# A two-tile head load moved to GpSimd's queue, and the key weights one place forward

## The chip, the cores and the metric

The kernel runs on one core of one Trainium2 chip. A core has a matrix engine (TensorE, PE in the profile; its weight loads are the row PEld), VectorE (DVE), ScalarE (ACT), GpSimd (POOL) and SyncE (SP), each with an instruction stream of its own. They meet through semaphores. Data come from device memory (HBM) into on-chip memory (SBUF, 128 partitions) by transfers that SP, ACT or POOL issue, each on a queue of its own; sixteen DMA engines of the core carry out what is queued. The results of matrix products lie in PSUM, eight banks.

The metric is the time of one execution on the device, in microseconds (us); each figure is the median of several runs. The profile is one further execution, recorded by the hardware profiler.

## The reference

Two layers follow one another on an input of 2048 tokens by 512 features: linear attention with 32 heads, then a gated unit that mixes along the tokens. The change touches what comes first, the layer norm of the input and the key product.

```python
def _A_ref(x, wqkv, wo):
    qkv = (x @ wqkv).reshape(B, S, 3, H, Dh)     # q, k, v of 32 heads
    pq, pk = phi(q), phi(k)                      # phi(t) = (t + 1 if t > 0 else exp(t)) + 1e-6
    kv, z = einsum('bhsd,bhse->bhde', pk, v), einsum('bhsd->bhd', pk)
    o = einsum('bhqd,bhde->bhqe', pq, kv) / (einsum('bhqd,bhd->bhq', pq, z) + 1e-6)
    return o.reshape(B, S, D) @ wo

def _B_ref(x, w_in, w_sp, b_sp, w_out):
    z = gelu(x @ w_in)
    z1, z2 = z[..., :Fh], layernorm(z[..., Fh:])
    return (z1 * (w_sp @ z2 + b_sp)) @ w_out

h  = x + _A_ref(layernorm(x), wqkv, wo)
h2 = h + _B_ref(layernorm(h), w_in, w_sp, b_sp, w_out)
```

## The kernel before

The program is written as a list of operations. Each has an engine, the tensors that it reads and writes, an estimated cost and, for a transfer, a latency until it lands (`lat`). From the tensors the program derives which operation waits for which; `soft` entries add an order for the planner alone. The order of all operations is not worked out while the kernel is built: it is a permutation, stored as the compressed string `ORDER`. Each engine runs its own operations in the order in which that string has them, and waits (on semaphores) where another engine or a transfer has to be done first.

The input has 16 tiles of 128 tokens. In the head of the program, `k_unit(n)` takes two tiles at a time: statistics on DVE (L544, L545; tile 1's on ACT instead, `ACTS`), the reciprocal root of the variance on ACT (`rstd_act`, tiles 0, 2 and 3) or on POOL (`rstd`, `rpow`), the normalization into `xn` (L589 on DVE for tiles 0 to 5), the transposition, the key product with `wqkv[:, :, D:2D]` into a PSUM bank, `phi` on ACT and DVE into `pk`, and then the product of `pk` with `xn` (L693), which is summed over all tiles. Tiles 0 to 3 are transposed on PE (L603, with `ident` as the operand, then copied by ACT into `xnT`), later ones by transposing transfers on SP's queue. Until tile 0 is there, PE runs products of the zero tile `warm` (L627). `q_unit` (the query product, L435) is placed between the key units; the first one stands after those of tiles 0 to 3.

The order on each engine at the head, as `ORDER` has it:

- SP: loads of tile 0, tile 2, `wka` (key weights, the upper half of the input features), tiles 4 and 5 (one load), tiles 6 and 7, tiles 8 and 9, `wq` (query weights), tiles 10 and 11, then transposes and the other loads.
- ACT: loads of tile 1, tile 3, `wkb` (the other half of the key weights); the load of the exp table (L532); two passes over tile 1 (`sh`); Ln and Exp for tile 0, then for tiles 2 and 3; four copies to `xnT` (tiles 0, 3, 2, 1); `phi`.
- POOL: the memsets of `warm` (L472) and `ident` (L473), the other constants (among them `epst`, which ACT's Ln reads, and `expo`), then small operations for the statistics.
- DVE: statistics of tiles 0, 3, 2; normalization of tiles 0, 3, 2, 1; statistics of tiles 5, 4, 6, 7, with `phi` from tile 0 on among them.
- PE: warm-up, transposes of tiles 0, 3, 2, the key product of tile 0, the transposes of tile 1, the key products of tiles 2, 1, 3, the L693 product of tile 0, the first query product.

`first_load` (L507) makes a head load; its argument `behind` makes the issuing engine wait until another load has landed. So the load of tiles 6 and 7 waits on SP for tile 2 (`x2`), and that of tiles 8 and 9, with those from 10 on, for `wkb` (`wk`).

Of the kernel before, what the change touches and what calls it, by code (L numbers as in the profile page):

```python
# [1261 lines left out]
```

## Time and profile before

| | |
|---|---|
| median of 3 runs | 223.34 us (223.34 to 223.61) |
| the profiled execution | 223.98 us, of which the span is 222.2 |
| granted TensorE clock | 1.0 throughout |
| data moved | 27.12 MB, mean 122 GB/s |

The profile is read from several views. The page gives the busy time of each engine. The chain of waits follows the work that ended last back from the last instruction: at each step to what released it. The timeline lists instructions in order of time, with the idle time in front of each and its releaser in brackets; an engine's name with a q (SPq, ACTq) is its sequencer, which issues transfers. The view of transfers gives for each issue the time until it landed. A table by stretches gives the busy time of each engine and, at its end, the granted clock, the busy share of the DMA engines and their traffic.

### The profile page before, as it was taken

The numbers are of one execution on the slowest core, as the hardware profiler recorded it, in microseconds if no ns is written. First come the engines' busy times: TensorE is split into PE (matmuls) and PEld (weight loads), VectorE is DVE, ScalarE is ACT, GpSimd is POOL, SyncE is SP. The second block draws the span as 40 slices with busy tenths as digits, with TensorE's granted clock in tenths as the row PEclk, the third lists the DMA queues.
The fourth block names the chain that finished last, engine by engine and source line by source line (L and its number), as shares of the span: only waits on it lengthen the run. The fifth ranks groups of instructions, "written<-read, shape, count | busy, mean of one in ns | idle before, by whom it ended". The sixth has DMA issues, their size and how long they took to land.

```text
span 222.2 us, 3893 instructions
## 1 busy us (share of the span) xinstructions
PE 215.9 (97%) x1346; PEld 125.5 (56%) x1358; DVE 207.1 (93%) x484; ACT 142.7 (64%) x283; POOL 49.7 (22%) x133
## 2 busy tenths in 40 slices
PE   8999999999999999999999999999999999999995
PEld 8543444343343554454455556756767798767764
DVE  3899759989998999999999999999999999999995
ACT  5778663277998999999856447626284459423330
POOL 3354500000573693885620000000000000000000
PEclk9999999999999999999999999999999999999999
DMA  6658778965747536303992552998563200433564
GB/s 193 217 121 236 170 167 196 236 137 131 142 101 139 118 71 122 71 0 78 195 139 78 160 126 43 182 189 115 107 119 67 41 1 3 83 73 59 111 190 155
DMA packets 75027, 27.12 MB, mean 122 GB/s; under 512 B 64768, under 2 KB 75008, under 8 KB 75008
## 3 DMA queue, kind: packets, MB, share of 16 engines
q1 hardware_dynamic: 74304, 26.30, 55.9%
q10 hardware_dynamic: 704, 0.59, 0.8%
q8 instruction: 10, 0.16, 0.3%
q14 instruction: 9, 0.07, 0.1%
HBM read 6.95 MB, written 2.10 MB: 41 GB/s over the span
## 4 chain that ended last, share of the span: by engine, by line
PE 79%; DVE 9%; DMA 5%; ACT 3%; SPq 2%; issue 1%; DVEq 0%
PE psum L435 73%; PE psum L693 5%; DMA x<-in_A_x_dram 3%; DVE st L544 2%; DVE pqT L620 2%; DMA zgT<-z1t 1%; DMA r<-rcp 1%; SPq L786 1%; ACT sh L454 1%; ACT e L454 1%; DVE e L615 1%; DVE us L756 1%; DVE h L1198 1%; DVE pqT L810 1%; SPq L465 1%
## 5 line engine op out<-in xcount | busy, mean ns | idle before, releaser
L454 ACT ACTIVATE psum<-psum 128x448 f32<-128x448 f32 (+2 forms) x79 | 32.3, 424 | 29.2 <-PE psum L435 22.7
L435 PE MATMUL psum<-z,wt 128*128 128x448 bf16 (+1 forms) x216 | 41.5, 335 | 0.1
L435 PEld LDWEIGHTS psum<-z,wt 128*128 128x128 bf16 x216 | 20.9, 98 | 15.4 <-ACT z L454 0.3
L435 PE MATMUL psum<-win,hnT 128*128 128x448 bf16 x112 | 25.8, 353 | 0.0
L454 ACT ACTIVATE e<-psum 128x1024 bf16<-128x1024 f32 (+1 forms) x18 | 16.7, 927 | 9.3 <-PE psum L435 8.7
L454 ACT ACTIVATE z1t<-psum 128x448 bf16<-128x448 f32 (+1 forms) x24 | 16.4, 682 | 9.5 <-PE psum L435 8.1
L454 ACT ACTIVATE p<-psum,b 128x448 f32<-128x448 f32 x24 | 14.7, 640 | 6.6 <-PE psum L435 4.2
L435 PE MATMUL psum<-ws,hs 128*128 128x448 bf16 x72 | 18.4, 353 | 0.0
L435 PEld LDWEIGHTS psum<-win,hnT 128*128 128x128 bf16 x112 | 10.7, 98 | 10.4 <-ACT z L454 0.3
L435 PE MATMUL psum<-zt,sa 128*128 128x448 bf16 (+1 forms) x92 | 16.3, 316 | 0.0
L693 PE MATMUL psum<-pk,xn 128*128 128x512 bf16 x62 | 15.4, 380 | 0.3 <-DVE pk L618 0.2
L435 PE MATMUL psum<-xnT,wqkv 128*128 128x512 bf16 x63 | 15.3, 379 | 0.3 <-DVE pqT L620 0.2
L435 PE MATMUL psum<-wqkv,xnT 128*128 128x512 bf16 x62 | 14.9, 379 | 0.7 <-ACT xnT L454 0.4
L435 PE MATMUL psum<-m,pqT 128*128 128x512 bf16 x62 | 14.8, 380 | 0.6 <-DVE pqT L810 0.4
L454 ACT ACTIVATE z<-psum 128x896 bf16<-128x896 f32 x16 | 14.9, 957 | 0.0
L888 DVE TENSOR_TENSOR psum<-psum,p5z 128x448 f32<-128x448 f32 x24 | 14.9, 623 | 0.1
L1038 DVE TENSOR_TENSOR u<-psum,p 128x448 bf16<-128x448 f32 x24 | 14.6, 617 | 0.4 <-ACT p L454 0.2
L568 POOL TENSOR_SCALAR st<-st 128x1 f32<-128x1 f32 x10 | 6.9, 691 | 34.1 <-ACT sh L454 32.6
L544 DVE BATCH_NORM_STATS2 st<-x 128x6 f32<-128x512 bf16 x15 | 9.8, 678 | 4.1 <-DMA x<-in_A_x_dram 4.0
L435 PE MATMUL psum<-wout,zgT 128*128 128x256 bf16 (+1 forms) x72 | 13.0, 297 | 0.1
L435 PEld LDWEIGHTS psum<-zt,sa 128*128 128x128 bf16 x92 | 8.9, 98 | 5.0
L454 ACT ACTIVATE sh<-h 128x512 bf16<-128x512 bf16 x16 | 10.0, 626 | 1.6 <-DVE h L858 1.3
(158 smaller groups left out, 463.7 us busy)
## 6 DMA issues: line engine op xcount, KB each, us to landing
r<-rcp SPq DMA_DIRECT2D x16, 128.0 KB, 2.7
out_dram<-h SPq DMA_DIRECT2D x15, 128.0 KB, 1.8
win<-in_B_w_in_dram SPq DMA_DIRECT2D x4, 448.0 KB, 3.8
x<-in_A_x_dram SPq DMA_DIRECT2D x6, 256.0 KB, 3.7
wqkv<-in_A_wqkv_dram SPq DMA_DIRECT2D x2, 512.0 KB, 4.9
wout<-in_B_w_out_dram SPq DMA_DIRECT2D x1, 896.0 KB, 5.2
wt<-in_B_w_sp_dram SPq DMA_TRANSPOSE x32, 3.7
wo<-in_A_wo_dram SPq DMA_DIRECT2D x1, 512.0 KB, 6.5
```

The costliest lines, as they stand in the source:

```text
L435: inst = pe.matmul(out_ap, lhsT=a, rhs=b, start=start and i == 0, stop=stop and i == len(pairs) - 1, **kw)
L454: return g.add("ACT", lambda ac: ac.activation(out_ap, in_ap, func, **kw), [in_ap, *extra], [out_ap] + ([accum] if accum is not None else []),
L465: return g.add(eng, lambda q: q.dma_start(out_ap, in_ap), [in_ap], [out_ap], cost=issue, lat=lat, dma=name, **k)
L544: dve(lambda v: v.bn_stats(s[:, 0:6], src[:, n, :]), [src[:, n, :]], [s[:, 0:6]], D)
L568: pool(lambda p: p.tensor_scalar(s[:, 2:3], s[:, 0:1], s[:, 0:1], -1.0 / (n * n), op0=ALU.mult, op1=ALU.mult), [s[:, 0:1]], [s[:, 2:3]], 240)
L615: dve(lambda v: v.tensor_scalar(e, e, 1.0, EPS_PHI, op0=ALU.min, op1=ALU.add), [e], [e], w * GW, acc=4)
L620: dve(lambda v: v.scalar_tensor_tensor(dst, t, 1.0 + EPS_PHI, e, op0=ALU.add, op1=ALU.max), [t, e], [dst], w * GW, ps=True)
L693: inst = pe.matmul(bank(CB[c]), lhsT=xn[:, i, c * P:(c + 1) * P], rhs=pk[:, i, :], start=i == 0, stop=i == NT - 1)
L756: return dve(lambda v: v.tensor_tensor(out_ap, a, b, op), [a, b], [out_ap], n, acc=2)
L786: g.add("SP", lambda q: q.dma_start(dst, src_ap), [rcp[:, i:i + w, :]], [dst], cost=700, lat=2200, dma=f"r{tg}{c // 2}")
L888: dve(lambda v: v.tensor_tensor(half(b), half(src), p, ALU.add), [half(src), p], [half(b)], HW, ps=True)
L1038: dve(lambda v: v.tensor_tensor(u, half(b), p, ALU.add), [half(b), p], [u], HW, ps=True)
```

## The change

Tile 2 and tile 3 were two loads of 128 KB, one on SP's queue and one on ACT's. They become one load of both tiles (256 KB) on POOL's queue. It is issued after the memset of `warm` and before that of `ident`. The halves of the key weights thereby become the second load on SP's queue and on ACT's. The load of tiles 6 and 7, which waited on SP for tile 2, waits for the new load. The estimated latencies of the three loads are set anew, and `ORDER` is stored anew for a program of one operation less. Read engine by engine, the new string has the same order as the old one on all five engines, but for the loads named. The two strings are left out here.

```diff
-    queue = {"SP": [], "ACT": []}
+    queue = {"SP": [], "ACT": [], "POOL": []}
...
     load_x("SP", 0, 1, 2150)
     load_x("ACT", 1, 1, 2300)
-    x2 = load_x("SP", 2, 1, 2300)
-    load_x("ACT", 3, 1, 2550)
-    first_load("SP", wqkv[:, 0:2, D:2 * D], A_wqkv[0:2 * P, D:2 * D], "wka", 4200)
-    wk = first_load("ACT", wqkv[:, 2:4, D:2 * D], A_wqkv[2 * P:4 * P, D:2 * D], "wkb", 4400)
+    x2 = load_x("POOL", 2, 2, 3000)
+    x2.soft.add(0)
+    g.ops[1].soft.add(x2.i)
+    first_load("SP", wqkv[:, 0:2, D:2 * D], A_wqkv[0:2 * P, D:2 * D], "wka", 4400)
+    wk = first_load("ACT", wqkv[:, 2:4, D:2 * D], A_wqkv[2 * P:4 * P, D:2 * D], "wkb", 4600)
     for n, lat, behind in ((4, 4600, None), (6, 3400, x2), (8, 3850, wk)):
         load_x("SP", n, 2, lat, behind)
```

More of the change, by code (lines that the diff above doesn't have):

```diff
@@ L15 @@
 SEM_NS = 45.0
-ORDER = "c-jrtg92EG76ibvyXVHXZQE&_G`4Nqww=bdZCh<@+qU)Ie8ogGvj_%@XOS(Eg|JW-)uNcpEv`i~T38D#q=mEimc$ZRUW;x?Eukf{+?LD|TRux}c`TLXw-lDz{<4%-*wR=5D`GJ$trfJQmce3L9V=w9td^y-VwT?OT5W4>^(>QRwEC9C+FEhTY}u@lWwplE#@bm4%W2uIy*03smcu$&1#4*ith9BszpbK$w*J=H%2+82V*@Ogb+SrU)?!;#8)#jus|~WsHrT3J73*e0th!CKq1M#G+dnqK;#d=#WHs!%4YSF%)TUTD8);LmnboxNHqC}xbDM76ZJD*OS=Pg5*lb&DEv=_5vAwq3W?Cy-VY{uDjkcB6+iuz_TWzCkt?jctw#NF{ej8&4Y_6@dLpIjt*g+d-hwX;-wRv{L#@kVwZ|iM=9kUI#&9-5qZMR#t$)4K;duTgsvn{kow$qN=F8kN6+G9Iw*X%!gV)yKfJ+l+G$j;eG+hV(L-Y(h&+iI8WlwGzf_S8PuJ3DP3?WcXRP>6+J_SIfkfNvHXzbynlTU3NZ9DK28AmSo4;sJ<`KNbebV2FXR_+j@gDZ(Kp!Xr5%A_7t)624nxq(K5iL0Y6hUN}-B1L7ke(xE7X^vI7?NQjK6fWJ@-1#s6Aqbw4kAS$8|>YzB1pb|163re6h{zhSBML85fNn}G^ltO)!M`q+gJJdrPR7OrzK?C$fTU133ltwi)M0@l?c2q|{bihcIL2op|RvbZN)WTOZK@HSK9vnqej6r{NL^I^ZzvzSA7>nuXgzXrG0T_p6=!}|}fzcR<Sr~-on2F`+g4?zdT`?Og@C^qr2Q9D)$1oS)aS(Sg7(MVG4q*t6qbF|TFz(?8PGCIlpd04lBv#{<b;o=>z$vuE1pLH9tieRw$4hI4UzmhP7>bMd2e0ihUSSw6Av@RNG~U<(T*f-QMh;%Vdi=&hyuonf<W$7x2>ihrkZ<iRoM(}XSFr&*AihHa#w8e%0ncF(ax)&MAr#N!2@-KKj3Jnqc{l~3`4kCx4Plss&#(lMxft(}hDjNPJ-8WRxe-zM0eRV-oA4278I7M%h!>EKJ$W6^k)KOZm(lqG1(=?n(VO8Ig9TZe`52z{xCOnKfj3ZxG5HrGurP}<BX1%Z8?YFQFe2--A^Wg6V=)t7q8v*wHXE@oTd^OLvoUwFKg%-(cQ7;m<}I{l7FOUcM&dlC<QEKPDpq70?q(d8WLs9^K$hYj4&V@0W@!%M9Jb?pmf<kYWoi!PUJmC%E?^aA<v})KRgT~yR^xkS;{=XmQ!eICyk#>k;Y6-xa~@%P-m!OV!8IJk4qVEPoWuwAfz>&hYxxhC@gqC&Gh6Z#$8Zl0aWdC&ESK{OSMUVab3exME2r=~zi}mxas&V4K5pbx{@^A~<0}5-FHUD!{>uaW&CcA+V;s-JoWXs7w(t+P@g7abN!4H>on;r!<W@?v7|3;or+JDYbdt3gTIp0>A$6BE8A@Gwf#(=T7uk&u8CJ9T-ooh;BPqPD@;oo|4)5~{3oC-I@e%hTqP8=#9<Y|KGm4_=F{A1RpD?<fvW8-)vSMjJW9k|E`%T7H9o=Fa#Z^_^W<ABzb0$=L<=0ClP;S*!BIQwH{iUQzqGEc*;!39adcnVyTqTrO4V6+UR6r$_UJX=AsnkfNRYYl&T18bxnN(Zll}}~WSmktD71Tr(m0fjJNlo>dQ`ADu)Irr$MH$snv(#EM)KLS}MsHY9T{OtEYL$AbliDk-)+n>Os;@U!XJt@7AEcSyO}*4gvwV(bs-3!PuGVRw2CIj9Yo2CnzJ{o+a%r{tXs9-8qh@<Hh4roaPup}t!?Z~|)K?qSPbalN!?jSOG(w9M&bMo%wrIU}YJm6GE{)bQ?bc$A(H;%<oEod4zE{h&L=pU7E!94))P9}PI8D?+t<ZQy^huhar;6kUbVmQ^xXvoE=g?Xm(@~w%R6S8-&!WS6tV4?L=XFaTbwS~Mnr`c&j%c!`>xC{UnSat%UDgnPscX8UE4rbt`l4^TtNZ$)S9-1Qx~X6Ktb6*Y<o-a{^;^UInf{3W{Qnhrt4De$IXv(vKF0_8aDS&%KEji_`v*n!ydKR*d1?>k(S3}M^t2ws(|8IW?HfJ4r}VL&&U1T0pWqpMl8^Hwp2f%eWY6eRe4=OdO#Y9@^tqndbND=;=Gi>EPxnn8+vj^M&+oZ>q5tIzJf|=AIKIg9cma>=3A~^$@xq?SL-<l}=J7nF7xH|*%$NIn74el`!OQvzU*&JK+DrHvFY4=ktN-oAe4DrMI$qq@d2`?HrF@6)_MKkRH+yN{<rV#;@9}cJ#cTV1ujHY9uh;d19>y#CK0o6B`F%g^Q~iM-@Roka%lm0R=4br4*Yh%d*8lYre%{Y{6~E{gyuP>cOa9$k`zgQdKfH}!^@o1NuX_V;>+QX&H}rOX%WwKMzu}Mlu0Qc=e#fi(FMsMC{F%@2NB-QS1YNv_zwoa9(rbB5Z{)AMyZ7+d-qRcVTYuy4y`wkrrvB02`BCrWpZtTz3_AN~|LtG=kAL;G-pwtD8f@@h9xF&2L<?dEy**CQ$KwVJ;s*%g1u=r#?m_e*L7*UAaL*G5LGaU)2H!kkkUR(#qzDoP>4Pvqh#*{$GDs4H4?+gXf($`~AXSh$2pwb$(gb0H%t53eQxGx85=0KN2LA)Me2vi"
@@ new lines @@
+ORDER = "c-jTQ0{|EY5Cp)zz5Up>ZQHgQHnwdxwr!)a)7Z9c+h%8gNQi)lFvLX&gn~mLA|ndIB0xxlLsY~;JS0Xm#77<^K?3ALLL@~ZBtu^0MoJ_{KBPb@<VRtoMsyTF5yU_m6hv(lMS8?UA=E-z)Il-)jaEp9x~PYYXoC#Mj7(^V;>d!mXoS{iixOyuY{-H7Xpd6Jjs~cRzUY852#u2Hgi7d#Fer;yD2<Nz2c3}<l~E2=(H~tf097y$)$kX(Vh{$SI>w_3!Xq{&Vi>NWF(#k}hF}twU^phDJf@%~nxX=RVk)Mg8M<L6mZCYPqdR6{5n7-J7GoD?U>RECU+h3njKp%>KrgJoN{qm2tio>WL~rcDDD1@?tifpP$3D!)7#zTL^ua;Q#aJA|Jgmih9L73qu`O7S|8Nr<@Bq&+4qLGi3-A!za0J_N1xIlek8lQeaSV@f8c(s^j$<Lt;siF~94_EIHsc~r;u0?73Etx^PT>Q7;3Gm>O#6bLcn;ZD{6Z`X>=U9`2#al>5!KA%SSX8YuxR!hp)INXL39ga-*FE~EUd+_aF)y>Sa?fi5$ziyS!#=Kku8lSw>;*S!qQtj%WG+^sL|3{K1*o{EQ3|F{8r2g*c}wKL{`ocS|O`swXL`%wh~s^GFoOUX|1fVm9i{W-bz~$%W8G3o>j0+mebl=YpY^)Er<PO^{uM4u|AgFs#zIpVAU;~wX>eq*BV+`Yj4A?k@d38*4PeO6RTw%?2FZ~ruMhxwnH|``dLTIWxegF?Xb}{&Hl50Y=n)mPPWwgTTPp8BW-|nwwcz<y4Va`X1B21X4${?)%MzKYi=v-u+6b=w$JX^K<jSDY>@4@Bi6%i*#Wz2-)*cNx4CxPy4pNDVJqz=##uMJZzrvV{jgQ`z{cAIyJs)Z(tg@RduW60g1y2cTWv3Gz74U9mW^xdl)c7UyJQROm1XB;`(>wXsJ*r`mV@hTipAqF`)$TIcw=YHdCqe3ifuLWt;J^?f*~j_v|OBOaT$`2Eg>h_9}76y5-~SJ@rfniReNfonV5?$5*OJ!OU)#V%<kN1VYuF+@V(_>H*T;GmWEOJ(F*arJ+rjz!E2U}OYFJTVKf$CI)>#Z>&0-4&P{gR3Nk$ZW?tT~y6nmHtj!3F!Tc=DqRhagjLG^e##k)EdThYnOvd8O$mD!s<(Y{k*oO_7nJw9ujo6Rdn1U6Ul3RJxO0pFzG9tHgE=%#V4P<FnVr!ORS?*wLwqa%V=Re%ZL9D_7oXxhJ$01C`IULNP+{Fd_i}RU<Rk@FiIgATgjqjM1<2am6xQN@VDc`Ue7jryUvN;d39pCacR&fN|a|t_e0^jpKs&gb)vm+;RDL?QNTW}OVa;NR*Xinl9F5_qZ%P~C8wcKN0xSW&ujbFKrhj@&;xt>$_of|lnEBJ%c_>+5Cjz{^68`+76IhF@Fox5!l;lH_scln1$XkLSb{0uvD1~-#FlXCadJjIg?`~+(;lvnq(9>VXiCPR7`p66MH_6zLF2b{$){tjXNA|rY@KgTP)#M`{gdo1kX{VE@FmqqaZ7|HLmmS1CJkLr&Y#jo=*qxloo@aSH}WBMM(@Tcsj8;s?({U+mhY_ICKSl8qFGbZqOp3h$}zUT6qp3rl9BG2zhJh2z^mn`l{y`Dd3Nl)e_JdZc<6rS7*cqvck^}V#G^oCx>i+E~J<wd=$XY{|lg6H*e-pI@QDX-{_J)2kZI$qhE_$yBK=HArXdj_xOe|Za^>8*Uazh(#j$6I?r@9bH8fL3@9@96D3jc4*z-o^W<nWy(o-d6*BhPrxBZ|O5N+h=%N@8)xSjraHNKG1vlT%YChe2};CoW9a~`(WSb>wT88dKhi?W4^_Y`w-vYTfL93^S*w<=lf7!;3IsPFZ8hb&xiXaU+dfaANBL?KGK)^4qxP>e5Vgo4j=7<wab_JVh^vQzQlL?azE*Ne2kCxeg3bH^$42a<NS$7)LuXB6a9#v@kGk*tNpMa^0Pk0AA2Na_5=RN_j^2@^PB#`&wDsc^;>?y5BemZ=Fk12C)G#4;+K4oUiekN?U((!fAP=$)$jN{|L!mSm4EXa{?kACT~DSTe&4V8FCU_({@YE@{Exr!hyK7RNQ$i4>aU@C>nSx%N#uI(QItnfHA1NrQqeR@!<9zSm0HO)QtOpYDKuJXl}iaUPU$s4i8V%<HCB_9L6bFJS(H%|6+?5BN!c}5Q<Y6wHBB27OY;;{`IJ)&lwb3eLyHt!3zb_16i4w@P>WSq2^DCGnkueBsF3n%sg~)T7twN6R5|^t*S<n4RYI#&RBN?aB~?sY)LgYyTx--!|EaXLYKOL|ls2l2wyTm(Xs60+lm6BoRaPkNQXPfXK2_0f9n>-1(*aG<eeG2X?N<ez(qWy}5!F>$9n~2f*EyZlU%H_4s;8E^sBdbele(nuYOO1Jpv$_Z`f8(gs;UNRtDCx^tGcd7x}$1(tlO%tpL(M9daCJqsAq~CbXE;LR~NldE!9**y;L`K*DLi<BfZgUy;BD@Rug^DTOCqIebjr!2s-JLe(AG*>x)*atNtiTuueS{Ge{Fe4Ppho6g%jxIDrN60t9h`=)o;{5G{xwqzxF{RiZ$_4<!k{DnXDe2pOack_QQc&_NJ{4N?S&gK$BJAZd_32p^;jQU#%c3_<E3Opqyv7-S401et?KL6+cu*CLIX"
```

## The prediction

> **What bounds the kernel now.** I read the page first, then the chain of work that ended last, then the timeline of the first 18 us engine by engine, then the landing times of the loads issued there, and last the traffic in stretches of 1 us.
>
> ```profile
> span 222.2 us, 3893 instructions
> ...
> PE 215.9 (97%) x1346; PEld 125.5 (56%) x1358; DVE 207.1 (93%) x484; ACT 142.7 (64%) x283; POOL 49.7 (22%) x133
> ```
>
> TensorE (PE) is busy for 215.9 of 222.2 us, so a change to four loads can only move the point from which that stream runs. The chain shows where this point is set (columns: start, duration, what):
>
> ```profile
> 0.79 0.39 SPq L465
> ...
> 1.25 0.41 SPq L465
> ...
> 2.17 5.98 DMA x<-in_A_x_dram
> ...
> 8.18 1.29 DVE st L544 x2
> ...
> 17.42 1.47 PE psum L435 x6
> ...
> 21.04 1.73 PE psum L435 x8
> ```
>
> From 17.42 us on the chain is PE's, and what starts it is VectorE's (DVE) work from 8.18 on, which waited for tiles 4 and 5 (issued at 2.17, landed at 8.15). A delay or a gain at 17.42 reaches the end whole, since what follows is dependent work with no load of fixed time in it. Eight matmuls take 1.73 us there, so PE can begin one every 0.216 us.
>
> The head itself, by the timeline (start, duration, what, and in brackets the idle time before it with its releaser):
>
> ```profile
> 0.78 0.20 POOL L472 MEMSET warm<- 128x128 bf16 x1 [0.29 <-POOLq L1247]
> 0.93 0.20 POOL L473 MEMSET ident<- 128x128 bf16 x1
> ...
> 1.24 0.45 ACTq L465 DMA_DIRECT2D x<-in_A_x_dram  x1
> ...
> 1.71 0.43 SPq L465 DMA_DIRECT2D wqkv<-in_A_wqkv_dram  x1
> 1.72 0.46 ACTq L465 DMA_DIRECT2D wqkv<-in_A_wqkv_dram  x1
> ...
> 2.03 0.27 POOL L492 TENSOR_SCALAR_AFFINE_SELECT selm<-selm 128x32 bf16<-128x32 bf16 x1
> ...
> 3.96 0.18 DVE L545 BATCH_NORM_AGGREGATE st<-st 128x2 f32<-128x6 f32 x1
> 4.07 0.37 SPq L465 DMA_DIRECT2D x<-in_A_x_dram  x1
> 4.26 1.29 DVE L544 BATCH_NORM_STATS2 st<-x 128x6 f32<-128x512 bf16 x2
> ...
> 4.88 0.28 ACT L454 ACTIVATE rs<-st,epst 128x1 f32<-128x1 f32 x1
> ...
> 5.68 0.38 DVE L589 TENSOR_SCALAR xn<-x,st,rs 128x512 bf16<-128x512 bf16 x1
> ...
> 6.35 1.20 PE L603 MATMUL psum<-ident,xn 128*128 128x128 bf16 x12
> 6.37 1.06 DVE L589 TENSOR_SCALAR xn<-x,st,rs 128x512 bf16<-128x512 bf16 x3 [0.31 <-ACT rs L454]
> ...
> 7.02 0.60 ACT L454 ACTIVATE xnT<-psum 128x512 bf16<-128x512 bf16 x1 [0.69 <-PE psum L603]
> ...
> 7.94 0.81 PE L435 MATMUL psum<-wqkv,xnT 128*128 128x512 bf16 x3 [0.39 <-ACT xnT L454]
> ...
> 9.60 0.66 DVE L544 BATCH_NORM_STATS2 st<-x 128x6 f32<-128x512 bf16 x1
> ...
> 9.67 1.89 PE L435 MATMUL psum<-wqkv,xnT 128*128 128x512 bf16 x8
> ...
> 11.76 1.04 PE L693 MATMUL psum<-pk,xn 128*128 128x512 bf16 x4 [0.19 <-DVE pk L618]
> ```
>
> Two strands run here. **Strand one**: the statistics of tiles 3 and 2 (4.26, in that order on DVE) stand ahead of tile 0's normalization (5.68), so the landing of tile 3 sets tile 0's transposes (6.35), its copy (7.02), the first key matmul (7.94) and the last of the key matmuls (the eight from 9.67). **Strand two**: the landing of tiles 4 and 5 sets DVE's stream from 8.18. The strands meet at PE's matmuls of 11.76, which wait for DVE's keys. PE's last key matmul begins at 9.67 + 7 x 0.216 = 11.18, so PE could go on at 11.40 and has 0.36 us to spare; DVE, idle from 6.37 + 1.06 = 7.43 to 8.18, has 0.75. As the profile stands strand two is ahead by those 0.36 us.
>
> Landing times, each row from the stretch around its issue (last figure: us from issue to landing):
>
> ```profile
> x<-in_A_x_dram ACTq DMA_DIRECT2D x1, 128.0 KB, 3.0
> ...
> wqkv<-in_A_wqkv_dram SPq DMA_DIRECT2D x1, 256.0 KB, 5.7
> wqkv<-in_A_wqkv_dram ACTq DMA_DIRECT2D x1, 256.0 KB, 5.9
> ...
> x<-in_A_x_dram SPq DMA_DIRECT2D x1, 256.0 KB, 4.8
> ...
> x<-in_A_x_dram SPq DMA_DIRECT2D x1, 256.0 KB, 2.7
> ```
>
> Tile 3, issued at 1.24, landed at 4.24, and DVE took it at 4.26. The key weights landed at 7.41 (SP's half) and 7.62 (ScalarE's, ACT's); tile 0's copy ended at 7.02 + 0.60 = 7.62. The 4.8 is tiles 6 and 7 (issued at 4.07, when tile 2 had landed), the 2.7 tiles 8 and 9.
>
> ```profile
> 1.00:2.00 1.00, 0.95 (x10) 0.96 (x11) 0.00 (x0) 0.00 (x0) 0.85 (x9) 1.00 0.10 32
> 2.00:3.00 1.00, 1.00 (x12) 1.00 (x11) 0.00 (x0) 0.80 (x1) 0.30 (x2) 1.00 1.01 327
> 3.00:4.00 1.00, 1.00 (x12) 1.00 (x10) 0.73 (x2) 0.99 (x2) 0.00 (x0) 1.00 0.85 230
> 4.00:5.00 1.00, 1.00 (x12) 1.00 (x11) 0.88 (x3) 0.97 (x5) 0.00 (x0) 1.00 0.88 286
> 5.00:6.00 1.00, 1.00 (x12) 1.00 (x11) 1.00 (x4) 0.57 (x3) 0.74 (x3) 1.00 1.10 365
> ...
> 7.25:8.25 1.00, 0.61 (x8) 0.45 (x7) 0.25 (x2) 1.00 (x3) 0.00 (x0) 1.00 0.07 25
> ```
>
> The last two columns are the DMA engines' busy share and GB/s. Traffic starts just before 2.0 and the engines are then full; but from 7.25 to 8.25 a share of 0.07, one engine of sixteen, is all that runs. So the late landing of tiles 4 and 5 is one engine's backlog, not a lack of bandwidth: by 6.0 us 32 + 327 + 230 + 286 + 365 = 1240 kB had moved of the 1311 kB that end with tile 5. Without that engine's delay they would have landed before 7.43 and strand one would lead.
>
> **The change part by part.** *Removed:* the second issue on SP's queue and the second on ACT's (0.41 and 0.45 us). The key weights move from 1.71 to 1.25, the load of tiles 4 and 5 from 2.17 to 1.71, and ACT's table load begins as much earlier. None of this buys anything by itself: the first key matmul waits for tile 0's copy as much as for the weights; tiles 4 and 5 pay only while strand two leads, 0.36 at most; ACT's work after the table load waits for tile 1, and what it makes is first needed by DVE behind tiles 3 and 2.
>
> *Added on GpSimd (POOL):* one issue between the memset of warm and that of ident, at about 0.95. Behind it stand ten short setup instructions, done at 2.03 + 0.27 = 2.30. Their first users are ACT's Ln at 4.88 (epst) and PE's transposes at 6.35 (ident), so an issue of up to 2.5 us stays covered; without that cover each us more would cost a us on tile 0. The memset of warm, which PE's warm-up waits for, stays ahead.
>
> *Moved behind the pair:* on SP the load of tiles 6 and 7 waits for tile 2, from now on for the pair, and behind it stand the loads of tiles 8 and 9, the query weights, and all later loads and transposes. Issued at 4.8 rather than 4.07 and landing 2.7 to 4.8 later, it is there at 7.5 to 9.6; DVE wants it at 9.60 plus the shift. Nothing.
>
> *The pair itself* is the term that decides. Before, tiles 2 and 3 stood ahead of the key weights in the same two queues; after, they share the engines with them. No row shows a load from POOL's queue, so I bound it. **Below:** DVE is busy with tile 0 until 3.96 + 0.18 = 4.14, so the pair cannot be used over 0.10 sooner than 4.24. **Above:** the nearest rows are 256-KB loads in the same crowd, 4.8 and 5.9, which give 0.95 + 4.8 = 5.75 and 6.85. **Taken:** the three queues carry 262 kB each (tile 0 and half of SP's weights' traffic; the same on ACT; the pair). Shared in thirds all is moved when 786 kB have passed: at 327 GB/s from 2.0 (32 kB before it) 2.31 later, at 4.31; at the traced rates (589 kB by 4.0, then 286) at 4.69. The lag to the landing is that of tile 3: 524 kB had passed at 3.0 + 165/230 = 3.72, it landed at 4.24, 0.52. So 4.8 to 5.2. I take 4.8, since the dip between 3 and 5 falls on a time when two queues changed from one load to the next and a third would fill it. That is 0.56 later than 4.24.
>
> *The Trainium skill speaks against the change here.* Its page "DMA: Bandwidth & Descriptors" (section "Latency and other measured facts") gives a load issued by GpSimd a first byte after about 1 us, one by the other two queues about 0.6; the trace has 1.2 for the latter (0.79 to 2.0), and no run here shows the former. By the page's difference the pair would land at 5.2, an estimate, and the time would be 224.3.
>
> **The sum.** The profiled execution took 223.98 us, 222.20 of it the span. Strand one moves by +0.56. In an execution like the profiled one 0.36 of it goes into PE's spare time (and DVE starts at 7.43 + 0.56 = 7.99, where tiles 4 and 5, due 0.46 earlier at 7.69, no longer hold it): +0.20, 224.18. The median of the runs shown is 223.34, 0.64 below the profiled execution; one without the lagging engine would be 0.36 below it, so I hold that the timed ones mostly lack it. There strand one leads already and the whole +0.56 shows: **223.34 + 0.56 = 223.9**. With the late landing in the timed runs too: 223.34 + 0.20 = 223.54.
>
> **The rivals.**
>
> *The pair is served first.* If POOL's queue gets half of the traffic rather than a third, 262 kB at 327/2 GB/s from about 2.15 are through at 3.75, landed at 4.27: +0.03, no change, 223.3 (223.0 where the late landing is typical and 0.33 of it are saved). For it: nothing stands ahead of the pair in its queue. Against: SP and ACT shared the time evenly, their key weights issued together landing 5.7 and 5.9 later. The skill's same page ("Queues, rings and completion order") says that an engine goes round the queues by whole packets, of some 9 to 17 descriptors; a queue with larger packets would then get more than its third, which no row here can show.
>
> *The faster side: the key weights are what PE waits for.* They land at 7.62, when tile 0's copy ends. If in the timed runs the lagging engine holds them past 7.62 by 0.46 or more, and the pair is not later than 4.24, then PE's first key matmul gains the whole 0.46 by which both halves are issued earlier, and tiles 4 and 5 come with it: 223.34 - 0.46 = 222.9. For it: the two ends coincide within the rows' rounding. Against: it needs the timed runs to lag more than the profiled one, which is the longer one.
>
> *POOL's queue is slow.* If making the transfer's descriptors on POOL, or its place in the crowd, takes as long as tiles 6 and 7 took, the pair lands at 5.75: +1.5, 224.85; with the 5.9 of the weights 6.85: +2.6, 225.95. For it: these are the only 256-KB loads in a full stretch. Against: one lagging engine made them late.
>
> **How the numbers follow.** Forecast 0.46, pair served first 0.21, weights 0.16, slow queue 0.17. About 0.2%, 0.45 us, is what a measurement of this kernel can tell, so slower begins at 223.79. The forecast's own range is 223.5 to 224.3, from the late landing's 223.54 to the skill's and the traced rates' 4.69 + 0.52 = 5.21; I give 0.33 of its 0.46 to slower, the rest to the same. Slower is 0.33 + 0.17 = 0.50; the same 0.13 + 0.21 + 0.02 = 0.36; faster 0.14. The range of 223.0 to 225.0 takes in the forecast, the first rival and the nearer half of the slow queue.
>
> **What would show it.** The statistics of tiles 3 and 2 begin at about 4.8 instead of 4.26, tile 0's normalization at 6.24, the first key matmul at 8.5; the key weights land well before that; DVE has no wait for tiles 4 and 5; PE's matmuls of 11.76 begin without a wait on DVE. Statistics at 4.3 or sooner would be the first rival, a first key matmul released by a load the second, statistics past 5.6 or a setup instruction of POOL holding up ACT's Ln the third. Another order of magnitude in the head, or a difference that arises behind 17.42, would make the whole reading wrong.

## The result and the profile after

| | before | after |
|---|---|---|
| median, same chip | 223.48 us (4 runs, 223.34 to 224.14) | 226.63 us (4 runs, 226.50 to 227.76) |
| ratio, 95% interval | | 1.0138 (1.0119 to 1.0157) |
| the profiled execution, its span | 223.98, 222.2 | 226.50, 224.8 |
| mean granted TensorE clock | 1.0 | 0.992 |

The change costs 3.15 us (226.63 - 223.48), where the forecast was 0.56 and the range ended at 225.0.

The chain of waits of the changed kernel, in order of time (start, duration, what):

```profile
0.79 0.20 POOL warm L472
0.99 0.34 issue
1.33 5.14 DMA x<-in_A_x_dram
...
6.50 1.28 DVE st L545 x2
...
10.34 1.49 PE psum L435 x3
...
12.25 1.93 PE psum L435 x8
...
14.20 0.61 ACT e L454
...
19.23 1.24 DVE pqT L621
...
20.51 1.47 PE psum L435 x6
```

The load in the chain is now the pair, 5.14 us from issue to landing, and the point from which PE's stream runs has gone from 17.42 to 20.51: +3.09. On the way there the chain now passes through PE's key products (10.34 and 12.25) and ACT's `e` (14.20), where before it ran on DVE. Behind the point nothing is lost. From this point to the end of the span it takes 224.8 - 20.5 = 204.3 us, and 222.2 - 17.4 = 204.8 before.

The timeline of the changed kernel's head, from the answers for POOL, DVE, PE and ACT:

```profile
0.79 0.20 POOL L472 MEMSET warm<- 128x128 bf16 x1 [0.29 <-POOLq L1248]
1.33 0.94 POOL L465 DMA_DIRECT2D x<-in_A_x_dram  x1 [0.34 <-issue]
...
3.41 0.27 POOL L492 TENSOR_SCALAR_AFFINE_SELECT selm<-selm 128x32 bf16<-128x32 bf16 x1
...
6.50 1.28 DVE L545 BATCH_NORM_STATS2 st<-x 128x6 f32<-128x512 bf16 x2 [2.20 <-DMA x<-in_A_x_dram]
...
9.59 1.28 DVE L545 BATCH_NORM_STATS2 st<-x 128x6 f32<-128x512 bf16 x2
...
13.41 0.29 DVE L616 TENSOR_SCALAR e<-e 128x512 bf16<-128x512 bf16 x1 [1.15 <-ACT e L454]
...
14.83 0.29 DVE L616 TENSOR_SCALAR e<-e 128x512 bf16<-128x512 bf16 x1 [0.19 <-ACT e L454]
...
8.36 0.40 PE L604 MATMUL psum<-ident,xn 128*128 128x128 bf16 x4 [2.16 <-DVE xn L590]
...
14.86 1.03 PE L694 MATMUL psum<-pk,xn 128*128 128x512 bf16 x4
...
12.29 0.60 ACT L454 ACTIVATE xnT<-psum 128x512 bf16<-128x512 bf16 x1 [1.48 <-PE psum L604]
```

DVE takes the pair at 6.50 instead of 4.26. The statistics of tiles 4 and 5 (9.59) have no wait in front of them any more: their load is there in time. In exchange DVE waits 1.15 and 0.19 us later on, for ACT's `e`, and ACT had waited 1.48 for PE. On PE, 14.86 - 8.36 = 6.50 us lie between the first transposes and the first L694 product; before it was 11.76 - 6.35 = 5.41. What slowed PE is in the table by stretches (stretch, its length, busy time of PE, PEld, DVE, ACT, POOL, then granted clock, DMA share, GB/s):

```profile
2.50:4.50 2.00, 2.00 (x22) 2.00 (x20) 0.88 (x2) 1.41 (x4) 1.03 (x10) 1.00 1.05 344
6.00:8.00 2.00, 0.20 (x4) 0.02 (x1) 1.50 (x5) 0.00 (x0) 0.73 (x2) 1.00 0.13 38
...
9.00:10.00 1.00, 0.92 (x8) 0.92 (x10) 1.00 (x4) 0.66 (x2) 0.00 (x0) 0.54 0.87 229
10.00:12.00 2.00, 1.78 (x9) 0.90 (x8) 2.00 (x6) 0.81 (x2) 0.74 (x2) 0.50 0.90 293
12.00:13.00 1.00, 1.00 (x7) 0.47 (x5) 0.25 (x1) 0.71 (x2) 0.16 (x1) 0.75 0.22 78
```

The warm-up products run out at 6.20, PE idles 2.16 us, and from about 9.1 to 12.5 it is granted half its clock. That is the whole of the mean of 0.992.

Landing times of the loads issued between 1.3 and 1.4 us, after:

```profile
wqkv<-in_A_wqkv_dram ACTq DMA_DIRECT2D x1, 256.0 KB, 3.8
wqkv<-in_A_wqkv_dram SPq DMA_DIRECT2D x1, 256.0 KB, 3.4
x<-in_A_x_dram POOLq DMA_DIRECT2D x1, 256.0 KB, 5.1
```

Queues (packets, MB, share of the 16 engines), after, first from 2.3 to 4.5 us, then from 4.5 to 6.0; q1 and q10 serve SP and ACT, q0 serves POOL:

```profile
q1 hardware_dynamic: 383, 0.36, 53.3%
q10 hardware_dynamic: 400, 0.39, 50.2%
...
q1 hardware_dynamic: 248, 0.24, 48.2%
q0 software_dynamic: 80, 0.26, 46.2%
q10 hardware_dynamic: 16, 0.01, 1.5%
```

From 2.3 to 4.5 the engines are full (share 1.05 in the stretch above) and q0 moves nothing at all, though its issue had ended at 1.33 + 0.94 = 2.27. The key weights, which nobody needed before the copy of tile 0, get the bandwidth and land 3.4 and 3.8 after their issue, where 5.7 and 5.9 had been needed before. The pair's whole 0.26 MB follows from 4.5 on.

### The profile page after: what moved, and what is told of

Read it like the earlier page. It is cut to its first block, busy times and chain, and to the rows that moved or that the text cites. A ratio compares the mean times of both kernels' runs of the same rounds, so it can differ in the third digit from the quotient of the medians.

```text
span 224.8 us, 3892 instructions
## 1 busy us (share of the span) xinstructions
PE 216.7 (96%) x1346; PEld 126.0 (56%) x1358; DVE 207.4 (92%) x484; ACT 142.6 (63%) x283; POOL 50.4 (22%) x134
## 4 chain that ended last, share of the span: by engine, by line
PE 83%; DVE 10%; DMA 4%; issue 1%; ACT 1%; POOL 0%; DVEq 0%; POOLq 0%
PE psum L435 76%; PE psum L694 5%; DMA x<-in_A_x_dram 2%; DVE pqT L621 2%; DMA zgT<-z1t 1%; DVE st L545 1%; DVE e L616 1%; DVE h L859 1%; DVE pqT L811 1%; ACT e L454 1%; DVE us L757 1%; PE psum L604 1%; DVE h L1199 1%; DVE pqT L619 1%; DVE pk L621 1%
## 5 line engine op out<-in xcount | busy, mean ns | idle before, releaser
L435 PE MATMUL psum<-wqkv,xnT 128*128 128x512 bf16 x62 | 15.8, 396 | 0.6 <-DVE pqT L621 0.3
L694 PE MATMUL psum<-pk,xn 128*128 128x512 bf16 x62 | 15.4, 379 | 0.1
L616 DVE TENSOR_SCALAR e<-e 128x1024 bf16<-128x1024 bf16 (+1 forms) x18 | 7.1, 395 | 5.5 <-ACT e L454 5.5
```

Of the source, the lines that this page charges most:

```text
L435: inst = pe.matmul(out_ap, lhsT=a, rhs=b, start=start and i == 0, stop=stop and i == len(pairs) - 1, **kw)
L616: dve(lambda v: v.tensor_scalar(e, e, 1.0, EPS_PHI, op0=ALU.min, op1=ALU.add), [e], [e], w * GW, acc=4)
L694: inst = pe.matmul(bank(CB[c]), lhsT=xn[:, i, c * P:(c + 1) * P], rhs=pk[:, i, :], start=i == 0, stop=i == NT - 1)
```

## The experiments

The theory at this point (A in the expectations) has two parts: the pair lands late because POOL's queue gets its turn only when the two other queues have let go, and the late pair leaves PE idle long enough to lose its clock, which costs again. The rivals: that the order alone (weights ahead of the pair) does it, on any queue; that POOL's queue is slow whatever else runs, or only at its first use; that the clock is a companion and costs nothing. Further letters in the expectations name such rivals where they were set down. All edits leave the other operations of each engine in their order; where an edit moves or removes an operation, `ORDER` is stored anew. The cuts below leave out that string and, where an edit to the kernel before uses POOL's queue, the entry for it in `queue`, which is the change's own.

**The clock apart from the landing.** Against the changed kernel, PE's warm-up products are made to last until the pair's tiles are normalized:

```diff
-second = warmup(16, 60, op)
+second = warmup(54, 60, op)
```

> The changed kernel with PE's second warm-up of 54 products instead of 16, so that PE works until tile 0 is there (about 8.4 us in the profile of the changed kernel, where PE stood idle from 6.2 to 8.36 and the granted clock was then 0.5 from about 9 to 12.5). Theory A (the late pair costs twice: by DVE's wait of 2.2 us and by the lowered clock, at which the first key matmuls followed one another in 0.43 us instead of 0.216): the clock stays at 1.0 and the matmuls of L694 begin 1.0 to 1.3 us earlier than 14.86, the time falls from 226.6 to 225.3 or 225.6. Rival B (the slow matmuls lie beside a wait of DVE and ACT and cost nothing): 226.4 to 226.8.

Measured: 225.66 us (4 runs, 225.19 to 226.18), ratio 1.0093 (1.0071 to 1.0116) against 223.55 of the kernel before on that chip. The pair landed at 6.59, 0.11 later than in the changed kernel. PE's timeline:

```profile
8.48 0.40 PE L604 MATMUL psum<-ident,xn 128*128 128x128 bf16 x4 [0.27 <-DVE xn L590]
...
13.43 1.03 PE L694 MATMUL psum<-pk,xn 128*128 128x512 bf16 x4
```

and the stretch and the chain of the same kernel:

```profile
10.00:12.00 2.00, 2.00 (x13) 0.97 (x13) 2.00 (x6) 1.68 (x4) 0.62 (x2) 1.00 0.98 330
```

```profile
17.80 1.24 DVE pqT L621
```

```profile
19.08 1.47 PE psum L435 x6
```

With PE busy the clock stays at 1.00, the way from the transposes to L694 is 4.95 us instead of 6.50, and the point of PE's stream comes at 19.08 instead of 20.51. So the clock costs 1.43 us at that point, and the late pair by itself, against the profile of the kernel before, 19.08 - 17.42 = 1.66. The four runs show the same in two groups: spans of 223.5 and 223.6 us at a mean clock of 1.0, 1.8 above the median of 221.7 of the kernel before on that chip, and 224.2 and 224.4 at 0.999 and 0.998. The profiled one is of the second group: 205.1 us follow the point in it, 0.8 more than in the changed kernel. Where those arise is not settled.

**The same pair on another queue.** Against the changed kernel, one load of both tiles, but second on SP's queue, ahead of SP's half of the weights; ACT keeps tile 1 and its half:

```diff
-    x2 = load_x("POOL", 2, 2, 3000)
-    x2.soft.add(0)
-    g.ops[1].soft.add(x2.i)
+    x2 = load_x("SP", 2, 2, 3000)
```

> The changed kernel with the load of tiles 2 and 3 on SP's queue (second place, the first half of the key weights third there, the second half second on ACT's) instead of POOL's. Theory A (the path through POOL's queue is what makes the pair late, 3.2 us from issue to its first traffic): the pair lands at 4.4 to 4.9 and the time is 223.4 to 224.2. Rival C (the pair is late because the key weights, one place further forward, share the DMA engines with it): it lands at 5.5 or later, 224.8 or more.

Measured: 223.62 us (10 runs, one of them 225.78 at a mean clock of 0.992), ratio 1.0012 (0.9991 to 1.0032): no difference is seen, and the interval reaches from 0.2 us faster to 0.7 slower. DVE's first use of the pair in its timeline, and the point in the chain:

```profile
4.78 1.29 DVE L543 BATCH_NORM_STATS2 st<-x 128x6 f32<-128x512 bf16 x2 [0.29 <-DMA x<-in_A_x_dram]
```

```profile
17.25 1.47 PE psum L435 x6
```

This is the landing that the forecast had: a pair at 4.76, DVE's first use 0.52 later than before. The point of PE's stream even comes 0.17 earlier than in the profile of before, since tiles 4 and 5 land at 6.61 here. Joining two loads into one does no harm that these runs can tell.

**The order alone, without POOL.** Against the kernel before, tiles 2 and 3 stay on SP and ACT, but third, behind the halves of the weights:

```diff
-    x2 = load_x("SP", 2, 1, 2300)
-    load_x("ACT", 3, 1, 2550)
     first_load("SP", wqkv[:, 0:2, D:2 * D], A_wqkv[0:2 * P, D:2 * D], "wka", 4200)
     wk = first_load("ACT", wqkv[:, 2:4, D:2 * D], A_wqkv[2 * P:4 * P, D:2 * D], "wkb", 4400)
+    x2 = load_x("SP", 2, 1, 2300)
+    load_x("ACT", 3, 1, 2550)
```

> The kernel before with the halves of the key weights second and tiles 2 and 3 (still two loads on SP's and ACT's queues) third: the second half of the change alone, without POOL. By the bytes ahead of them (1.05 MB at 327 GB/s from 2.0, lag 0.5) tiles 2 and 3 land at 5.6 to 5.9, 1.4 to 1.7 later than before, and PE is idle for about 1.2 us. Theory A (the lateness goes whole into strand one, which has 0.36 to spare; the clock falls only after a longer idle time): 224.4 to 225.0. Rival B' (1.2 us of idle time already lower the clock): 225.3 to 226. If the time is within 0.4 of before, the landing of tiles 2 and 3 isn't what sets the head.

Measured: ratio 1.0113 (1.0073 to 1.0153), from runs of 224.76, 226.41 and 227.17 us, with mean granted clocks of 1.0, 0.992 and 0.991; a fourth run, 229.05 us at 0.984, is not in the ratio. The profiled one is the first:

```profile
6.17 1.29 DVE L544 BATCH_NORM_STATS2 st<-x 128x6 f32<-128x512 bf16 x2 [1.78 <-DMA x<-in_A_x_dram]
```

```profile
18.63 1.47 PE psum L435 x6
```

So putting the weights ahead of tiles 2 and 3 does most of the damage without POOL's queue: DVE starts at 6.17. Here PE idled 1.47 us, and the clock was kept in the profiled run, which had 18.63 - 17.42 = 1.21 us of loss at the point, and lost in the three others. What two of them paid on top, 1.7 and 2.4, is of the size of the clock's share above; the fourth paid 4.3.

**Which part of the pair's 5.14 us is POOL's.** Against the changed kernel, both halves of the weights on SP, the first held until tile 0 has landed, so that little else is queued when the pair is issued:

```diff
-    load_x("SP", 0, 1, 2150)
+    x0 = load_x("SP", 0, 1, 2150)
...
-    first_load("SP", wqkv[:, 0:2, D:2 * D], A_wqkv[0:2 * P, D:2 * D], "wka", 4400)
-    wk = first_load("ACT", wqkv[:, 2:4, D:2 * D], A_wqkv[2 * P:4 * P, D:2 * D], "wkb", 4600)
+    first_load("SP", wqkv[:, 0:2, D:2 * D], A_wqkv[0:2 * P, D:2 * D], "wka", 4400, x0)
+    wk = first_load("SP", wqkv[:, 2:4, D:2 * D], A_wqkv[2 * P:4 * P, D:2 * D], "wkb", 4600)
```

> The changed kernel with both halves of the key weights on SP's queue and held until tile 0 has landed (3.4 us), so that from about 2.9, when tiles 0 and 1 are through, to about 4.5 nothing but the pair is queued. Theory A (the path through POOL takes its 3.2 us to the first traffic by itself): the DMA engines lie idle from 3.0 to 4.4, the pair's traffic starts at about 4.5 and it lands at 5.5 to 6.3. Rival C (in the changed kernel the weights and tiles 4 and 5 kept the engines from the pair): traffic goes on without a hole and the pair lands by 4.5.

Measured: one run, 224.98 us, of which the span is 222.2, as before; 2.8 us lie outside it instead of the 1.7 to 2.0 of most other runs, so the time says nothing. The pair's landing, the queues from 2.3 to 4.5 and the chain:

```profile
x<-in_A_x_dram POOLq DMA_DIRECT2D x1, 256.0 KB, 3.6
```

```profile
q0 software_dynamic: 77, 0.26, 44.8%
q10 hardware_dynamic: 140, 0.13, 16.6%
q1 hardware_dynamic: 123, 0.11, 14.5%
```

```profile
17.43 1.90 PE psum L435 x8
```

With less in its way the pair lands 3.6 us after its issue, at 4.95: between what the two theories gave it. The 1.54 that are missing from 5.14 are the competition of the other loads, and 3.6 is still 0.9 more than the 2.7 of tiles 8 and 9, the same size on SP's queue; most of that is the longer issue (0.94 us against 0.36). DVE takes the pair at 4.97, 0.71 later than before; tiles 4 and 5 are there at 8.04, just before DVE is free for them, and the point is where it was before.

Is the 0.9 the price of a first use? Against the kernel before, tiles 14 and 15 come by POOL's queue at 12.67 us, long after the head:

```diff
-    for n, lat in ((10, 4000), (12, 4200), (14, 4400)):
-        load_x("SP", n, 2, lat, wk)
+    for eng, n, lat in (("SP", 10, 4000), ("SP", 12, 4200), ("POOL", 14, 4400)):
+        load_x(eng, n, 2, lat, wk)
```

> The kernel before with the load of tiles 14 and 15 on POOL's queue, issued at about 13 us in the middle of POOL's work, not as the first transfer of the program. The same load took 2.7 to 3 us on SP's queue when little else was under way. Theory A1 (POOL's path is always slow): 4 to 5.5 us from issue to landing. Rival A2 (it is the first use that is slow): 3.5 or less.

Measured: one run, 223.43 us; the issue and the landing:

```profile
12.67 0.94 POOL L465 DMA_DIRECT2D x<-in_A_x_dram  x1
```

```profile
x<-in_A_x_dram POOLq DMA_DIRECT2D x1, 256.0 KB, 3.6
```

The same 0.94 of issuing and the same 3.6, with other transfers under way. So it is no effect of the program's start. Whether the first use of a queue costs something stays open: this load, too, is the first and only one on POOL's queue.

Is it the size? Against the kernel before, tile 3 alone (128 KB) goes to POOL's queue, and ACT's half of the weights thereby comes second:

```diff
-    load_x("ACT", 3, 1, 2550)
+    x3 = load_x("POOL", 3, 1, 2550)
+    x3.soft.add(0)
+    g.ops[1].soft.add(x3.i)
```

> The kernel before with tile 3 alone (128 KB) on POOL's queue; tile 2 stays second on SP's, the key weights come second on ACT's and third on SP's. Theory A (a fixed time before the first traffic, 3.2 us, whatever the size): tile 3 lands at 5.5 to 6.0, POOL's issue takes about half of 0.94 us. Rival D (the delay grows with the number of descriptors): issue and delay are halved, it lands by 4.8.

Measured: one run, 226.44 us, clock 0.992. Issue and landing:

```profile
1.32 0.77 POOL L465 DMA_DIRECT2D x<-in_A_x_dram  x1 [0.33 <-issue]
```

```profile
x<-in_A_x_dram POOLq DMA_DIRECT2D x1, 128.0 KB, 4.7
```

Half the bytes took 0.77 us to issue, more than half of 0.94, and landed at 6.04, just past what theory A gave; the point came at 20.20. It is not the size of the load, and one tile is about as bad as two.

**Other loads on POOL's queue.** Against the kernel before, tiles 4 and 5 go there:

```diff
+    x4 = load_x("POOL", 4, 2, 4600)
+    x4.soft.add(0)
+    g.ops[1].soft.add(x4.i)
-    for n, lat, behind in ((4, 4600, None), (6, 3400, x2), (8, 3850, wk)):
+    for n, lat, behind in ((6, 3400, x2), (8, 3850, wk)):
```

> The kernel before with tiles 4 and 5 (not 2 and 3) loaded by POOL's queue after the memset of warm; all else as before. Theory A (POOL's path takes 5.1 us from its issue at 1.3 whatever it carries): they land at 6.3 to 6.9, which is ahead of DVE's need at 7.43, and the time is 223.0 to 223.5: below before by up to 0.36 where the late landing of tiles 4 and 5 was typical, the same where it was not. Rival C (what shares the engines with POOL's load sets its landing): with three loads ahead in the other queues it lands past 7.5, 223.5 or more.

Measured: 223.58 us (12 runs), ratio 1.0007 (0.9990 to 1.0023). Tiles 4 and 5 landed at 7.29, between the two theories' times and 0.86 sooner than before, and DVE had no wait for them. But:

```profile
8.10 0.81 PE L435 MATMUL psum<-wqkv,xnT 128*128 128x512 bf16 x3 [0.55 <-DMA wqkv<-in_A_wqkv_dram]
```

The wait only moved: the first key matmul now waits for the weights.

The weights themselves, both halves as one load of 512 KB on POOL's queue, tiles 0, 2 on SP and 1, 3 on ACT (against the kernel before):

```diff
-    first_load("SP", wqkv[:, 0:2, D:2 * D], A_wqkv[0:2 * P, D:2 * D], "wka", 4200)
-    wk = first_load("ACT", wqkv[:, 2:4, D:2 * D], A_wqkv[2 * P:4 * P, D:2 * D], "wkb", 4400)
+    wk = first_load("POOL", wqkv[:, :, D:2 * D], A_wqkv[:, D:2 * D], "wka", 4400)
+    wk.soft.add(0)
+    g.ops[1].soft.add(wk.i)
```

> The kernel before with the key weights, both halves in one load of 512 KB, on POOL's queue after the memset of warm; tiles 2 and 3 second on SP's and ACT's queues as before, tiles 4 and 5 third on SP's. If a load by POOL starts at 4.5 and moves 350 kB a us, the weights land at 6.4 to 7.2, before tile 0's copy (7.6) wants them, and tiles 4 and 5 by 6, before DVE wants them at 7.43: neither strand waits, time 222.9 to 223.4, that is 0.1 to 0.5 below before. Rival: the weights land past 7.7 and PE's first key matmul waits for them as in the run with tiles 4 and 5 by POOL: 223.5 or more.

Measured: 223.79 us (12 runs), ratio 0.9995 (0.9976 to 1.0014). The weights landed 6.5 after their issue, at 7.79, where 7.41 and 7.62 had been: past 7.7, as the rival had it. PE's first key matmul followed at 7.93, about 0.1 after the transposes ahead of it, and DVE waited 0.30 for tiles 4 and 5, there at 7.97. A load that has slack can go to POOL's queue at no cost that these runs can tell; it wins nothing either.

**When does POOL's queue get its turn?** Two kernels were made for this, both against the changed one. In the first ACT's queue has tile 1 alone and SP's both halves of the weights, without a hold:

```diff
-    wk = first_load("ACT", wqkv[:, 2:4, D:2 * D], A_wqkv[2 * P:4 * P, D:2 * D], "wkb", 4600)
+    wk = first_load("SP", wqkv[:, 2:4, D:2 * D], A_wqkv[2 * P:4 * P, D:2 * D], "wkb", 4600)
```

> The changed kernel with the second half of the key weights on SP's queue too (third there, not held), so that ACT's queue carries tile 1 alone and is empty from about 3.1. In the changed kernel POOL's queue moved nothing from 2.3, when its issue ended, to 4.5, which is when ACT's queue ran empty; with the weights held it began at about 3.2. Theory E (POOL's queue gets its turn when one of the other two runs empty): first traffic at 3.1 to 3.5 and landing at 5 to 5.6, beside SP's loads. Rival F (it waits for what was queued before it, in whichever queue): first traffic at 4.3 or later, landing past 6.

Measured: one run, 226.79 us, clock 0.992. The queues from 2.3 to 4.5 us:

```profile
q1 hardware_dynamic: 421, 0.40, 56.1%
q10 hardware_dynamic: 142, 0.13, 16.9%
q0 software_dynamic: 17, 0.07, 9.6%
```

q0 began at 3.91, and the pair landed at 6.96 (5.6 after issue), later than in the changed kernel. Theory E's 3.1 to 3.5 is wrong, and so is rival F's 4.3 for the first traffic, though its landing past 6 came true. ACT's queue had been empty since about 3.1; q0 began when SP's first half of the weights, issued just ahead of the pair, was nearly through (it landed at 4.17), and from 3.8 to 4.2 the DMA engines' share was only 0.42. So POOL's queue need not wait until both others have nothing left, but an empty one is not enough, and it has no even share either.

The second puts the pair's issue ahead of POOL's memset of `warm` (in `ORDER`, and by this line for the planner):

```diff
     x2 = load_x("POOL", 2, 2, 3000)
-    x2.soft.add(0)
     g.ops[1].soft.add(x2.i)
```

> The changed kernel with the pair's issue ahead of the memset of warm, not behind it: POOL issues it at about 0.8 instead of 1.33 (PE's warm-up then starts 1 us later, so the time is not comparable). Theory G (a fixed time from issue, whatever else is queued, is part of the 3.2 us): the first traffic comes 0.5 earlier, at about 4.0, landing at about 6. Rival H (only the other queues' backlog counts): first traffic stays at 4.4 to 4.8. Third possibility: the descriptors are now there by 1.8, before the key weights' traffic, and the pair goes first: landing by 4.5.

Measured: one run, 227.13 us. The issue's row in POOL's timeline:

```profile
1.30 0.94 POOL L465 DMA_DIRECT2D x<-in_A_x_dram  x1 [0.80 <-POOLq L1247]
```

First in POOL's order, it begins at 1.30 instead of 1.33: 0.80 us of idle time stand in front of it. The issue was hardly moved, so this run decides nothing on the rule; it shows that even the first place in POOL's order does not bring the pair forward. The pair landed 5.6 after issue, at 6.90.

## Why the prediction was wrong

**What bounds the kernel** was read rightly: the change acted on the point at 17.42 alone, and its 3.09 there came through to the end.

**The direction** was right (slower was the likeliest), and the *late statistics* are what the third rival, "POOL's queue is slow", had set as its sign ("past 5.6"). Its two prices put the pair at 5.75 and 6.85; it landed at 6.48. The rival's mechanism, POOL's making of the transfer and its place in the crowd, is what the runs show, and I gave it 0.17 because "one lagging engine made them late". Its upper time, 225.95, lies 0.7 below the measured one; that it comes so near is in part luck, since it lacks the clock and does not take off DVE's idle time (both below).

**The step that failed is the landing of the pair**, taken as 4.8. Three parts of it were wrong:

| | forecast | measured |
|---|---|---|
| issue begins on POOL | 0.95 | 1.33 |
| first traffic of POOL's queue | 2.0, as on the others | 4.50 (3.21 with the weights held) |
| share of the traffic from 2.3 to 4.5 | a third | nothing |
| landing | 4.8 | 6.48 |

That the three queues share in thirds was the assumption with the greatest weight, and no row of the kernel before could show it. 1.33 + 2.7 + 0.9 + 1.54 = 6.47: the issue, a transfer of that size on SP's queue, POOL's own extra, and the competition. The last two are differences taken from the run with the weights held, so the sum divides the 6.48 and is no second proof of it.

The Trainium skill, in "DMA: Bandwidth & Descriptors", section "Latency and other measured facts", gives a load issued by GpSimd 0.4 us more to the first byte. With the weights held POOL's first traffic came 1.9 after its issue began and 0.9 after the issue had ended, where SP's and ACT's first traffic came 1.0 and 1.2 after their issues began; the measured extra to the landing is 0.9. The Trainium skill's same page, section "Queues, rings and completion order", has an engine go round the queues by packets. Here one queue stood still for 2.2 us while two others were full; 0.9 of that it took with the weights held too, and no run shows whether it had work ready in the rest, so that rule alone does not tell when the queue gets its turn.

**The spare time was read off the wrong engine.** "0.36 of it goes into PE's spare time" should have been DVE's 0.75. The chain of the run with the longer warm-up goes from the pair's landing through DVE to `pqT` at 17.80: DVE does the pair's statistics and normalizations and then those of tiles 4 and 5, and only its idle time of 0.75 before 8.18 takes up delay. The four profiles that keep their clock with a pair at least 0.5 us late bear this out:

| pair's statistics begin | later by | less 0.75 | measured at the point |
|---|---|---|---|
| 4.78 (on SP's queue) | 0.52 | -0.23 | -0.17 |
| 4.97 (weights held) | 0.71 | -0.04 | +0.01 |
| 6.17 (order alone) | 1.91 | 1.16 | +1.21 |
| 6.62 (longer warm-up) | 2.36 | 1.61 | +1.66 |

So against the profile of the kernel before, a pair less than 0.75 late is free. Against an execution in which tiles 4 and 5 come in time it is not: such a one had its point at 16.93 (below), and the pair on SP's queue comes 0.32 behind that. In the times the 0.56 of the forecast is neither shown nor excluded; the interval of the pair on SP's queue has room for it.

**A term was missing altogether: the clock.** PE's warm-up ends at 6.20, and nowhere does the prediction say what PE does between the end of the warm-up and late transposes. For the changed kernel the point is 2.24 later by the pair, less 0.75, makes 1.49; DVE's two waits for ACT's `e` (1.15 + 0.19 = 1.34), which the longer warm-up does not have, and 0.26, what is left and was not traced further, make up the rest of the 3.09.

**The reading of the 0.64 us** between the profiled execution and the median ("the timed ones mostly lack" the late load) is not settled. Two things cost the profiled execution of the kernel before about half a microsecond each. One is the late landing itself. The run with tiles 14 and 15 on POOL's queue has the same first loads; there tiles 4 and 5, issued at 2.19, landed at 7.51 instead of 8.15, DVE did not wait for them, and its chain reads

```profile
16.93 1.90 PE psum L435 x8
```

that is 0.49 before 17.42. The other is in the chain of the kernel before, at 63 to 68 us, a stretch on which I did not look:

```profile
63.27 1.83 SPq L786
...
65.14 2.81 DMA r<-rcp
```

There PE's stream waits for a transfer. From the point to the end of the span take 204.8 us in the kernel before, with the weights held and with the weights on POOL's queue, whose chains all have this wait, and 204.3 in the changed kernel, with the pair on SP's queue and in the order alone, whose chains lack it. (The run with tiles 14 and 15 lacks it and takes 204.8 all the same; its chain leaves PE between 76 and 132 us.) The timed runs of before may lack the one or the other: 23 of them on one chip have a median span of 221.7 us, 0.5 below the profiled 222.2, and they leave no trace that could tell which. The wait at 63 us also explains why the spans differ by 2.6 only, where the point moved by 3.09.

**What held:** the issue of POOL covered the setup instructions behind it (done at 3.68, ACT's Ln not held up); the weights came 2.5 to 2.8 us sooner (4.66 and 5.06) and bought nothing; the loads queued behind the pair cost nothing; DVE has no wait for tiles 4 and 5. The rival *pair served first* is out: POOL's queue had nothing until 4.50, and then 46% beside q1's 48%. The rival of the *key weights* as PE's wait did not come up in the changed kernel, but did as soon as tiles 4 and 5 were taken out of the two queues.

**Open:** by what rule POOL's queue gets its turn (it began at 3.21 with little else queued, at 3.91 with ACT's queue empty, at 4.50 beside two full ones), and at what idle time the clock falls. One pattern is in the traces, not tested by an edit of its own: in seven of the eight kernels with a load on POOL's queue in the head, its traffic began 0.3 to 0.9 us before the landing of the last load issued ahead of it on either of the other queues; with tiles 4 and 5 it began 0.4 after. No version tried beats the kernel before. Of the three that equal it over ten or more runs, two move the wait between the weights and tiles 4 and 5, and the pair on SP's queue trades a later pair for earlier tiles 4 and 5.

## What to carry to other kernels

A load that the first work waits for belongs at the front of a queue that starts early; asking how much of the bandwidth a newly used queue will get needs a run, not a division. Measure slack on the engine whose work the chain runs through, not on the one that waits at the end. And where an edit may leave PE idle, ask what keeps it busy: if nothing does, the idle time can be paid twice (here 1.66 us for the late pair and 1.43 for the clock).

## What the runs showed of the hardware

- POOL takes 0.77 us to issue a load of 128 KB and 0.94 for one of 256 KB, where SP and ACT take 0.36 to 0.51 for the first loads of the kernel before; and here its issue does not begin before 1.30 us even as the first operation in POOL's order.
- In the changed kernel POOL's queue moved nothing for 2.2 us after its issue had ended, while the queues of SP and ACT were full; with the weights held it was 0.9 us. Once it started it moved 0.26 MB in 80 packets, against 248 packets for 0.24 MB on q1: its packets are over three times as large, and it then had a share of 46%.
- An idle PE can lose its clock sooner than I had thought. After 2.16 us of idle time all four runs of the changed kernel had a mean clock of 0.992 (the idle times are those of the profiled runs). After 2.80 (both halves of the weights on SP's queue), 1.39 (tile 3 alone on POOL's queue) and 1.32 (the pair issued first) the one run of each had lost it too. After 1.47 (the order alone) the profiled run kept it and the three others lost it; after 0.98 (the pair on SP's queue) nine of ten kept it, and after 1.05 (the weights held) the one run did. So one gap of 1.47 passed and one of 1.32 did not. In the four profiles that lost it the half clock lasted 3.4 us, and it need not begin with the gap: with tile 3 alone it began at 9.8, 1.9 us after PE was at work again. The page "TensorE: Matmul & The Clock Gate" of the Trainium skill (section "HAM oscillation") tells to keep such gaps under about 3.4 us; by these runs 1.3 can already be too long.
